# Maxima, sums, division and layout of the early 256-query jobs by matrix products instead of transfers

## The chip, the cores and the metric

The kernel runs on one core of a Trainium2 chip. The metric is the device time of one execution in microseconds (us); the median of three executions of the kernel before is 1216.22 us (1215.47 to 1220.72). One execution was profiled; its trace is what is read below. The engines are TensorE (PE in the rows; PEld is its weight load), VectorE (DVE), ScalarE (ACT), GpSimd (POOL) and SyncE (SP, which only issues transfers here).

## What is computed

Decayed causal attention over 8 batches of 8 heads (576 positions, head size 64), followed by a feed-forward layer with a squared ReLU over the 4608 resulting tokens:

```python
scores = scale * np.matmul(q, k.transpose(0, 1, 3, 2))
cum = np.cumsum(np.log(np.clip(f, 0.0001, 1.0)), axis=-1)
decay = cum[:, :, :, None] - cum[:, :, None, :]
scores = np.where(causal, -1000000000.0, scores + decay)
scores = scores - np.max(scores, axis=-1, keepdims=True)
attn = np.exp(scores)
attn = attn / (np.sum(attn, axis=-1, keepdims=True) + 1e-09)
attn_out = np.matmul(attn, v)            # 8 x 8 x 576 x 64
x = attn_out.transpose(0, 2, 1, 3).reshape(4608, 512)
h = np.maximum(x @ w_in, 0.0)            # 512 -> 2048
out = h * h @ w_out                      # 2048 -> 512
```

All arrays are float32. Most matrix products run on operands split into an upper part (a reduced float32 that TensorE takes in one pass, `fp32r` in the rows) and a lower part (the rest), three products for one.

## The kernel before

**Attention jobs.** The work on attention is cut into jobs. The first eight are LOW jobs: job g takes the queries 0 to 255 of heads 2g and 2g+1 of batches 0 and 1. Then come 16 HIGH jobs (queries 256 to 575 of one head of these two batches), then 48 FULL jobs (a head of the other batches). A job loads q and k (`load`, L542), makes the split operands (`c1` to `c4`, `s1`, `s2`, L590 to L617), puts the cumulated decay in two more rows of the operands (`rows`, L561), and takes the row maxima: a matmul with the queries on the partitions (`mm`, L684, matmul L687) and a masked minimum of the negated scores on VectorE (`top`, L692, L695), one number for each query in a column of the tile `tcol`. The scores are then computed again with the keys on the partitions (`score`, L737, matmuls L739 and L743), where the maxima must lie along a row: `store` (L701, L704) writes the column `tcol` into row 66 of the operand by a transfer. ScalarE takes the exponential out of PSUM (`exp`, L749), GpSimd masks the diagonal block (`mask`, L752), and the products with v follow (`av`, L820; L824 for LOW jobs and batches 0 and 1, in full float32).

**Sums and division.** v has a column of ones, so row 64 of the product is the sum of each query, and the result lies transposed: 64 features on the partitions, queries along the row. ScalarE copies it to `xt` and the sums to `den` (L848, L854). For each pair of jobs `finish` (L889) then gathers the sums into a square tile by a transfer (`cmp<-den`, L901), inverts them on VectorE (L905, L906), stores them in DRAM (L909), spreads them over 64 partitions by two more transfers (L916) and multiplies (`divide`, L929).

**Feed-forward.** Chunks of 256 tokens: chunk c is split into `xh` and `xl` (`chunk`, L967; L977 and L983). Chunks 0 and 1 are the LOW queries of batches 0 and 1. For each of 16 slices of the hidden layer `mlp` (L1003) runs 12 matmuls (`m1`, L1020), ReLU (L1026), the square twice on two paths (`gh`, upper part, ScalarE L1035; `g`, L1030 on ScalarE or L1032 on VectorE), their difference (`gl`, VectorE L1038), and 6 matmuls (`m2`, L1049). While chunk 0 runs, chunk 1 runs beside it with the same slices. The 32 weight slices are loaded by GpSimd and split, mostly on VectorE (`weight`, L410: L427, L431, L438, L444, L309, L452); a slice can be used when its `lower` (L452) is done.

**What sets the order.** Every piece of work is recorded with `add`: its engine or engines with a planned duration, what it comes after, buffers that it takes and gives, and a priority. `Order.run` (L122) plays these durations through and emits the pieces in the order in which they would start; each engine then works through its own list strictly in that order. `SLACK` (L102) is added to the planned end of every piece before another may start on it. Where a piece can run on two engines, the one that would end first is taken (L149). `weight_prio` and `job_prio` set the priorities of weights and jobs, `SETS` and `RAWS` how many jobs may use operand buffers that lie in the place of later weight slices. The loads of q, k and v are issued by ScalarE (`QUEUE`), all other transfers of the attention by SyncE.

## Time and profile before

| | kernel before |
|---|---|
| median of three executions | 1216.22 us |
| the profiled execution: its time | 1220.14 us |
| its span, first to last instruction | 1218.4 us |
| TensorE busy | 1165.4 us (96%) |
| VectorE, ScalarE, GpSimd busy | 790.8, 724.4, 381.0 us |
| mean granted clock of TensorE | 0.983 |

Busy time leaves out the issuing of transfers and waits. The clock is a share of full speed. A group row gives the line of the kernel, engine, operation, output<-input by names, shapes and count, then the busy time in all, the mean duration of one (ns), and the idle time of the engine ahead of it with what ended it. Neighbouring instructions of an engine overlap a little at their ends, so the durations of a stretch sum to more than its busy time. The start of the run is where the engines wait most; from 250 us on TensorE hardly waits.

### The profile page before, as it was taken

To read this page: it belongs to the slowest core of one execution; us is meant where nothing else is said; L and a number is where in the kernel's file an instruction comes from. 1 tells how busy PE (TensorE), PEld (TensorE's weight loads), DVE (VectorE), ACT (ScalarE), POOL (GpSimd) and SP (SyncE) were. 2 spreads that over 40 slices of the span, in tenths; PEclk is the share of its full clock that TensorE was granted. 3 is DMA by queue.
4 is the path that set the end of the run, shared out by engine and by line. 5 is a ranking of instruction groups with operands and counts; after the bars stand their busy time and mean duration, and the time that the engine had idled before them with its cause. 6 is when DMAs were issued, how large, how long until landed. Compare 5 with 4: busy or idle time off the path is not lost.

```text
span 1218.4 us, 23217 instructions
## 1 busy us (share of the span) xinstructions
PE 1165.4 (96%) x7600; PEld 1038.7 (85%) x7600; DVE 790.8 (65%) x2211; ACT 724.4 (59%) x1859; POOL 381.0 (31%) x568
## 2 busy tenths in 40 slices
PE   4679998999999999999999999999999999999998
PEld 4558776789998898999999998899998999999997
DVE  7689988968877677777657674467656753233332
ACT  3566766556766666767777674477746763333232
POOL 3223321245444344544444442045423510000000
PEclk9689999999999999999999999999999999999999
DMA  3654554321222112222212212012211200000000
GB/s 80 140 129 121 143 154 113 87 77 43 65 50 62 40 41 59 47 64 47 59 42 59 42 43 58 19 41 43 69 31 44 47 28 11 18 19 11 8 19 18
DMA packets 122354, 69.85 MB, mean 57 GB/s; under 512 B 101914, under 2 KB 106042, under 8 KB 122234
## 3 DMA queue, kind: packets, MB, share of 16 engines
q10 hardware_dynamic: 53760, 31.47, 10.5%
q1 hardware_dynamic: 63866, 20.12, 7.5%
q0 software_dynamic: 4608, 16.78, 4.4%
q8 instruction: 61, 1.00, 0.3%
q14 instruction: 59, 0.48, 0.1%
HBM read 58.14 MB, written 9.88 MB: 56 GB/s over the span
## 4 chain that ended last, share of the span: by engine, by line
PE 85%; DMA 6%; DVE 4%; ACT 2%; issue 1%; POOL 1%; SPq 0%; ACTq 0%; POOLq 0%; DVEq 0%
PE bank L1049 31%; PE bank L1020 30%; PE bank L739 4%; PE bank L687 4%; PE bank L743 4%; PE bank L824 3%; PE bank L829 3%; PE bank L828 3%; PE bank L827 3%; DMA den<-rdr 2%; DMA cmp<-den 1%; DMA rdr<-cmp 1%; DMA up<-tcol 1%; DVE bank L695 1%; POOL pl L752 0%
## 5 line engine op out<-in xcount | busy, mean ns | idle before, releaser
L1049 PE MATMUL bank<-w,gh 128*128 128x512 f32 x1152 | 413.5, 400 | 1.9 <-DVE w L452 1.9
L1020 PE MATMUL bank<-xh,w 128*128 128x256 f32 x2304 | 324.4, 283 | 2.5 <-DVE xh L977 1.1
L1020 PEld LDWEIGHTS bank<-xh,w 128*128 128x128 f32 x2304 | 302.3, 189 | 13.7 <-DVE xh L977 1.3
L1026 ACT ACTIVATE r<-bank 128x256 f32<-128x256 f32 x288 | 110.2, 383 | 243.3 <-PE bank L1020 220.7
L1049 PEld LDWEIGHTS bank<-w,gh 128*128 128x128 f32 x1152 | 218.0, 189 | 41.8 <-DVE w L452 2.3
L1049 PE MATMUL bank<-w,gl 128*128 128x512 f32 x576 | 228.6, 397 | 0.3 <-DVE gl L1038 0.3
L1032 DVE TENSOR_TENSOR g<-r 128x256 f32<-128x256 f32 x191 | 82.9, 434 | 174.6 <-ACT r L1026 173.3
L1020 PE MATMUL bank<-xl,w 128*128 128x256 f32 x1152 | 182.0, 280 | 0.9 <-DVE xl L983 0.9
L752 POOL TENSOR_SCALAR_AFFINE_SELECT p<-p 128x128 f32<-128x128 f32 (+1 forms) x240 | 84.3, 353 | 307.3 <-ACT p L749 302.0
L695 DVE CUSTOM_DVE_ANT_0 bank<-bank,mz 128x448 f32<-128x448 f32 (+4 forms) x320 | 137.1, 431 | 66.5 <-PE bank L687 64.9
L780 DVE TENSOR_TENSOR pl<-p,ph 128x320 fp32r<-128x320 f32 (+3 forms) x240 | 147.9, 625 | 39.5 <-ACT ph L777 38.4
L1038 DVE TENSOR_TENSOR gl<-g,gh 128x256 fp32r<-128x256 f32 x288 | 139.6, 485 | 51.9 <-ACT g L1030 20.3
L1020 PEld LDWEIGHTS bank<-xl,w 128*128 128x128 f32 x1152 | 155.3, 189 | 1.3 <-DVE xl L983 1.3
L607 POOL TENSOR_TENSOR st<-qkraw,up 64x576 fp32r<-64x576 f32 x96 | 146.2, 1523 | 27.3 <-issue 5.4
L749 ACT ACTIVATE p<-bank 128x320 f32<-128x320 f32 (+4 forms) x288 | 110.0, 389 | 56.5 <-DVE pl L780 30.6
L739 PE MATMUL bank<-up 67*128 67x192 f32 (+3 forms) x364 | 121.8, 335 | 20.4 <-DMA up<-tcol 10.3
L1035 ACT ACTIVATE gh<-r 128x256 fp32r<-128x256 f32 x288 | 120.1, 417 | 31.6 <-PE bank L1049 11.6
L777 ACT CAST ph<-p 128x320 fp32r<-128x320 f32 (+3 forms) x240 | 106.2, 446 | 49.0 <-POOL p L752 27.6
L687 PE MATMUL bank<-up 66*128 66x448 f32 (+1 forms) x352 | 112.1, 322 | 13.0 <-DMA up<-w 9.9
L1049 PEld LDWEIGHTS bank<-w,gl 128*128 128x128 f32 x576 | 109.4, 190 | 15.1 <-DVE gl L1038 1.5
L743 PE MATMUL bank<-st 128*128 128x192 f32 (+3 forms) x364 | 109.3, 302 | 0.0
L739 PEld LDWEIGHTS bank<-up 67*128 67x128 f32 (+1 forms) x364 | 68.5, 188 | 31.5 <-DVE cmp L905 7.2
(102 smaller groups left out, 1612.5 us busy)
## 6 DMA issues: line engine op xcount, KB each, us to landing
qkraw<-in_qk ACTq DMA_DIRECT2D x48, 288.0 KB
v<-in_v ACTq DMA_DIRECT2D x64, 160.0 KB
out<-osb SPq DMA_DIRECT2D x35, 256.0 KB
w<-in_w_in POOLq DMA_DIRECT2D x16, 512.0 KB, 4.4
w<-in_w_out POOLq DMA_DIRECT2D x16, 512.0 KB, 4.6
den<-rdr SPq DMA_DIRECT2D x48, 144.0 KB
up<-tcol SPq DMA_DIRECT2D x232, 0.5 KB
qkraw<-in_qk ACTq DMA_DIRECT2D x11, 224.0 KB
```

The costliest lines, as they stand in the source:

```text
L607: (nc.vector if e == "DVE" else nc.gpsimd).tensor_tensor(out=out, in0=in0, in1=in1.bitcast(F32), op=ALU.subtract,)
L687: nc.tensor.matmul(ps.tile[:m, :n], r2[:D + 2, o + q0:o + q0 + m], kl0[:D + 2, o + k0:o + k0 + n], start=True, stop=True,)
L695: nc.vector.tensor_tensor_reduce(out=ps.tile[:m, :n], in0=ps.tile[:m, :n], in1=mz[:m, mo:mo + n], op0=ALU.add, op1=ALU.min, scale=-1.0, sc ...
L739: nc.tensor.matmul(ps.tile[:kn, :n], kl0[:D + 3, o + k0:o + k0 + kn], r2[:D + 3, o + q0:o + q1], start=True, stop=False,)
L743: nc.tensor.matmul(ps.tile[:kn, :n], l2[:, o + k0:o + k0 + kn], r1[:, o + q0:o + q1], start=False, stop=True,)
L749: nc.scalar.activation(out=pt.tile[:kn, :n], in_=ps.tile[:kn, :n], func=AF.Exp, scale=SCALE)
L780: nc.vector.tensor_tensor(out=pl.tile[:kn, :n], in0=pt.tile[:kn, :n], in1=ph.tile[:kn, :n].bitcast(F32), op=ALU.subtract,)
L1020: nc.tensor.matmul(ph.tile[:, :T], w[:, s, cc], x[:, cc, :], start=(cc == 0 and k == 0), stop=(cc == NCC - 1 and k == 2),)
L1026: nc.scalar.activation(out=r.tile, in_=ph.tile[:, :T], func=AF.Relu)
L1035: nc.scalar.activation(out=gh.tile, in_=r.tile, func=AF.Square)
L1038: nc.vector.tensor_tensor(out=gl.tile, in0=g.tile, in1=gh.tile.bitcast(F32), op=ALU.subtract)
L1049: nc.tensor.matmul(po, x[:, ts], w[:, s], start=(fc == 0 and k == 0), stop=(fc == NF - 1 and k == 2),)
```

## The change

For LOW jobs alone: the negated maxima go into the scores as products of a matrix of ones with a diagonal matrix (the identity `eye` scaled by the column `tcol`), one for each 128 queries. The products with v are turned round, so that queries lie on the partitions and sums in a column beside them; VectorE inverts the column, ScalarE (or VectorE) scales the rows, and a product with the identity turns the result back. `xh` and `xl` are taken from that in PSUM. For all jobs some choices of engine change, a favour of 300 ns against VectorE enters the choice, slacks and priorities are new, and SyncE instead of ScalarE issues the LOW jobs' loads of q, k and v.

```diff
-    SLACK = {"PE": 250.0, "DVE": 200.0, "ACT": 200.0, "POOL": 200.0, "SP": 200.0}
+    SLACK = {"PE": 300.0, "DVE": 250.0, "ACT": 250.0, "POOL": 200.0, "SP": 200.0}
+    FAVOUR = {"PE": 0.0, "DVE": 300.0, "ACT": 0.0, "POOL": 0.0, "SP": 0.0}
...
-                        if way is None or start + busy < way[0] + way[1][1]:
-                            way = start, w
+                        done = start + busy + self.FAVOUR[e]
+                        if way is None or done < way[2]:
+                            way = start, w, done
...
     def weight_prio(i):
-        return (14.9 if i < 4 else 16.9) + 0.8 * i
+        return (10.1 if i < 4 else 15.1) + 0.65 * i
...
-            return 12 + 2 * (g - NLOW)
-        return (30 if g < NLOW + BE * H else 98) + g - NLOW - H
-    SETS = 16
-    RAWS = 14
+            return 8 + 1.5 * (g - NLOW)
+        return (20 if g < NLOW + BE * H else 98) + g - NLOW - H
+    SETS = 14
+    RAWS = 16
...
+    DIRECT = 2
...
+    FIRST = "SP"
...
+    eye = rest[0][:, :P]
+    normal = spare_v.pop().rearrange("p i j d -> p (i j d)")[:, :2 * P]
+    small = spare(16)
+    ones = small[:, :P]
+    diags = [small[:, i * P:(i + 1) * P] for i in range(1, 8)]
...
-            add(("load", g), [dma(260000, QUEUE, 2)], load, [before("load") or "f"], take=[raw], prio=p - 4)
+            add(("load", g), [dma(260000, FIRST, 2)], load, [before("load") or "f"], take=[raw], prio=p - 4)
...
-            elif g == 0:
+            elif g < DIRECT:
...
+                if final and kind == LOW:
+                    dg = dgs[i, q0] = buf("diag", lambda x: diags[x])
+                    def diag(e, t=t, dg=dg):
+                        if e == "ACT":
+                            nc.scalar.activation(out=dg.tile, in_=eye, func=AF.Copy, scale=tcol.tile[:, t:t + 1])
+                        else:
+                            nc.vector.tensor_scalar(dg.tile, eye, tcol.tile[:, t:t + 1], None, ALU.mult)
...
+                if kind == LOW:
+                    nc.tensor.matmul(
+                        ps.tile[:, :n], kl0[:D + 2, o + k0:o + k0 + P], r2[:D + 2, o + q0:o + q1],
+                        start=True, stop=False,
+                    )
+                    for x in range(q0, q1, P):
+                        nc.tensor.matmul(
+                            ps.tile[:, x - q0:x - q0 + P], ones, dgs[i, x].tile, start=False, stop=False,
+                        )
+                    nc.tensor.matmul(
+                        ps.tile[:, :n], l2[:, o + k0:o + k0 + P], r1[:, o + q0:o + q1], start=False, stop=True,
+                    )
...
+    def low_products(g, p, pend, last_av):
...
+                for t in range(QA // P):
+                    for j in range(t + 1):
+                        nc.tensor.matmul(
+                            acc.tile[:, at(i, t)], pend[unit[i, j]][0].tile[:, (t - j) * P:(t - j + 1) * P],
+                            spare_v[g][:, i, j, :D + 1], start=j == 0, stop=j == t,
+                        )
...
+        def invert(e):
+            x = den.tile[:, :4]
+            nc.vector.tensor_scalar_add(x, view()[:, :, D], EPS)
+            nc.vector.reciprocal(out=x, in_=x)
+        def divide(e):
+            if e == "DVE":
...
+            for a in range(4):
+                nc.scalar.activation(
+                    out=out.tile[:, a * D:(a + 1) * D], in_=view()[:, a, :D], func=AF.Copy, scale=den.tile[:, a:a + 1],
+                )
+        def turn(e):
+            for t in range(QA // P):
+                nc.tensor.matmul(
+                    turned.tile[:, t * P:(t + 1) * P], out.tile[:, t * P:(t + 1) * P], eye, start=True, stop=True,
+                )
+        def upper(e):
+            copy(e, xs[b].tile[0][:, g % NPAIR, :], turned.tile[:, :QA])
+        def lower(e):
+            xh, xl = xs[b].tile
+            nc.vector.tensor_tensor(
+                out=xl[:, g % NPAIR, :], in0=turned.tile[:, :QA], in1=xh[:, g % NPAIR, :].bitcast(F32), op=ALU.subtract,
+            )
...
-                add(key, [act(n)] if c < 2 else [dve(n)], upper, need, take=[] if keys else [xs[c]], prio=p)
+                add(key, [act(n), dve(n)], upper, need, take=[] if keys else [xs[c]], prio=p)
```

How this moves the order is shown at three places. The names are those of the tiles; `up`, `st` and `w` hold the split operands (the w tiles are places of later weights), with a number that tells users apart.

On TensorE, where the first LOW job's scores begin, in the kernel before:

```order
L687 MATMUL bank_191<-up_71 128x128
L739 MATMUL bank_202<-up_71 128x256
L743 MATMUL bank_202<-st_77 128x256
L687 MATMUL bank_205<-up_72 128x256
L739 MATMUL bank_211<-up_71 128x128
L743 MATMUL bank_211<-st_77 128x128
```

and in the changed one, where w_86 is the tile of the ones and the diagonals:

```order
L715 MATMUL bank_195<-up_71 128x128
L779 MATMUL bank_202<-up_71 128x256
L784 MATMUL bank_202<-w_86 128x128 x2
L787 MATMUL bank_202<-st_77 128x256
L779 MATMUL bank_211<-up_71 128x128
L784 MATMUL bank_211<-w_86 128x128
L787 MATMUL bank_211<-st_77 128x128
```

The products with the diagonals stand between the two halves of each score, and no transfer of maxima comes ahead of them.

On SyncE's queue, right behind the load of f, before:

```order
L568 DMA up_71<-w_81 1x2x256
L568 DMA up_71<-w_82 1x2x256
L401 DMA cum_dr<-w_81 64x576
L401 DMA cum_dr<-w_82 64x576
L704 DMA up_71<-tcol_177 1x128x1 x2
L570 DMA up_72<-cum_dr 2x2x256
L704 DMA up_71<-tcol_177 1x128x1 x2
L570 DMA w_74<-cum_dr 2x2x256
L704 DMA up_72<-tcol_214 1x128x1 x4
```

and now, where L575 and L665 are the loads of q and k and of v:

```order
L575 DMA qkraw<-in_qk 64x2x256 x2
L575 DMA w_162<-in_qk 64x2x256 x2
L593 DMA up_71<-w_81 1x2x256
L593 DMA up_71<-w_82 1x2x256
L421 DMA cum_dr<-w_81 64x576
L421 DMA cum_dr<-w_82 64x576
L575 DMA w_177<-in_qk 64x2x256 x2
L593 DMA up_72<-w_81 1x2x256
L593 DMA up_72<-w_82 1x2x256
L575 DMA w_216<-in_qk 64x2x256 x2
L597 DMA w_74<-cum_dr 2x2x256
```

The transfers of maxima are gone from this queue, and the loads of later jobs now stand behind the decay rows of earlier ones.

On VectorE, where the sums of the second pair of LOW jobs are inverted, before:

```order
L695 ISA tcol_527 128x1
L929 TENSOR_TENSOR xt_326<-xt_326,den_357 128x2x256
L695 ISA bank_529,tcol_527<-bank_529,mz 128x256
L695 ISA tcol_527 128x1
L309 CAST w_81<-w_457 64x512
L905 TENSOR_SCALAR cmp_531<-cmp_531 128x8
L906 RECIPROCAL cmp_531<-cmp_531 128x8
```

and the first job's inversion, scaling and split now:

```order
L1009 TENSOR_SCALAR tcol_346<-bank_319 128x4
L1010 RECIPROCAL tcol_346<-tcol_346 128x4
L1014 TENSOR_TENSOR w_85<-bank_319,tcol_346 128x256
L723 ISA bank_362,tcol_364<-bank_362,mz 128x256
L723 ISA tcol_364 128x1
L316 CAST st_77<-w_297 64x512
L634 TENSOR_TENSOR st_77<-w_297,up_71 64x512
L723 ISA bank_372,tcol_364<-bank_372,mz 128x128
L723 ISA tcol_364 128x1
L634 TENSOR_TENSOR st_77<-w_297,up_71 64x512
L1035 TENSOR_TENSOR xl_385<-bank_366,xh_384 128x256
```

The inversion now reads the sums out of PSUM, once for each job, and waits for TensorE instead of for a transfer; other work stands between it and the split.

## Rows read from the trace of the kernel before

**Rows 1.** Slices of a fortieth of the span: busy tenths of TensorE, granted clock.
```profile
PE   4679998999999999999999999999999999999998
PEclk9689999999999999999999999999999999999999
```

**Rows 2.** Stretches (us): length, busy time of engines, clock, transfers' share, GB/s.
```profile
0.00:50.00 50.00, 27.00 (x110) 22.23 (x110) 36.16 (x108) 20.34 (x47) 14.77 (x48) 0.87 0.48 116
50.00:100.00 50.00, 39.23 (x203) 30.89 (x202) 41.48 (x114) 33.35 (x87) 12.38 (x31) 0.82 0.48 111
100.00:150.00 50.00, 48.62 (x288) 39.96 (x288) 46.31 (x114) 35.01 (x88) 18.04 (x28) 1.00 0.52 146
150.00:200.00 50.00, 44.35 (x261) 36.23 (x259) 40.11 (x101) 33.26 (x82) 13.32 (x29) 0.97 0.48 135
200.00:250.00 50.00, 46.35 (x259) 37.63 (x260) 45.74 (x124) 27.84 (x71) 13.58 (x22) 0.93 0.31 86
300.00:1000.00 700.00, 696.07 (x4794) 634.58 (x4794) 475.23 (x1372) 474.65 (x1237) 284.96 (x382) 1.00 0.21 48
1000.00:1219.00 219.00, 213.78 (x1369) 192.60 (x1367) 70.66 (x183) 67.98 (x166) 1.42 (x1) 1.00 0.04 14
```

**Rows 3.** The weights' lower parts: count, min/median/max ns, first and last start.
```profile
L452 DVE TENSOR_TENSOR w<-osb,w x32: 666/684/778, 55.3 to 247.4; 128x512 fp32r<-128x512 f32 x32
```

**Rows 4.** Waits of TensorE up to 140 us: in total, times, longest.
```profile
PE bank L739 <- DMA up<-tcol: 10.0, 4, 4.2
PE bank L687 <- DMA up<-w: 9.9, 1, 9.9
PE bank L739 <- DVE cmp L905: 6.6, 2, 4.8
```

**Rows 5.** Waits of VectorE up to 95 us.
```profile
DVE cmp L905 <- DMA cmp<-den: 8.5, 3, 4.1
DVE bank L695 <- PE bank L687: 3.8, 6, 1.0
DVE xt L929 <- DMA den<-rdr: 1.2, 1, 1.2
```

**Rows 6.** TensorE in order of time, first scores: start, duration, wait ahead.
```profile
14.88 0.55 PE L739 MATMUL bank<-up 67*128 67x256 f32 x1 [3.85 <-DMA up<-tcol]
```

**Rows 7.** VectorE by shape, up to 250 us.
```profile
L695 DVE CUSTOM_DVE_ANT_0 bank<-bank,mz 128x256 f32<-128x256 f32 x32 | 13.6, 425 | 10.3 <-PE bank L687 9.5 <-DMA up<-tcol 0.8
L983 DVE TENSOR_TENSOR xl<-xt,xh 128x256 fp32r<-128x256 f32 x12 | 5.0, 439 | 0.1
L309 DVE CAST w<-w 64x512 fp32r<-64x512 f32 x11 | 4.6, 414 | 0.2
L929 DVE TENSOR_TENSOR xt<-xt,den 128x512 f32<-128x512 f32 x4 | 2.7, 681 | 1.2 <-DMA den<-rdr 1.2
L905 DVE TENSOR_SCALAR cmp<-cmp 128x8 f32<-128x8 f32 x4 | 0.7, 185 | 8.5 <-DMA cmp<-den 8.5
```

**Rows 8.** ScalarE by shape, up to 250 us.
```profile
L749 ACT ACTIVATE pl<-bank 128x128 f32<-128x128 f32 x16 | 4.4, 276 | 2.2 <-PE bank L824 1.4 <-PE bank L743 0.5
L749 ACT ACTIVATE pl<-bank 64x64 f32<-64x64 f32 x15 | 3.2, 210 | 0.9 <-PE bank L743 0.8
L1030 ACT ACTIVATE g<-r 128x256 f32<-128x256 f32 x33 | 13.4, 406 | 1.5 <-DVE gl L1038 1.4
```

**Rows 9.** The same square on VectorE, whole span.
```profile
L1032 DVE TENSOR_TENSOR g<-r 128x256 f32<-128x256 f32 x191 | 82.9, 434 | 174.6 <-ACT r L1026 173.3
```

**Rows 10.** ScalarE and its queue's issues, in order of time: start, duration.
```profile
0.80 1.51 ACTq L550 DMA_DIRECT2D qkraw<-in_qk  x2
6.24 0.54 ACTq L550 DMA_DIRECT2D w<-in_qk  x1
9.87 0.62 ACT L309 CAST up<-w 64x512 fp32r<-64x512 f32 x1 [1.72 <-DMA w<-in_qk]
```

**Rows 11.** TensorE's last wait, in the last group of the feed-forward.
```profile
1212.36 0.19 PEld L1049 LDWEIGHTS bank<-w,gl 128*128 128x128 f32 x1 [0.35 <-DVE gl L1038]
```

More of the change, by code (lines that the diff above doesn't have):

```diff
@@ L458, in weight @@
         splits = ("c1", "c2", "c3", "c4", "s1", "s2")
-        if 17 <= i < 20:
-            after += [("avs", NLOW - 1)]
+        if 16 <= i < 20:
+            after += [("turn", g) for g in range(NLOW)]
         elif 20 <= i < 24:
@@ L759, in job @@
             need.append(("score", g, u - 1) if u else ("score", g - 1, len(jobs[g - 1]["units"]) - 1) if g else None)
-            add(("score", g, u), [pe(n, n)], score, need, take=[ps], give=[operands], prio=p - 0.3)
+            give = [dgs[i, x] for x in range(q0, q1, P)] if kind == LOW else []
+            add(("score", g, u), [pe(n, n, *[P] * len(give))], score, need, take=[ps], give=[operands] + give, prio=p - 0.3)
             add(("exp", g, u), [act(n)], exp, [("score", g, u)], take=[pt], give=[ps], prio=p - 0.5)
@@ L800, in job @@
             uses[u] = uses.get(u, 0) + 1
-        both = bank("av") if kind == LOW else None
         den = st["den"] = (
@@ L832, in job @@
             n = s1_ - s0
-            take = [acc] if first and (kind != LOW or i == 0) else []
+            take = [acc] if first else []
             give = [x for x in (ph, pl) if x]
@@ L836, in job @@
             need = need + [last_av] + ([("v", g)] if whole else [("vl", g)])
-            if whole and kind != LOW:
+            if whole:
                 need.append(("ones", g))
@@ L861, in job @@
                 m = QA if low else S - QA
-                take = [xts[b]] if h % H == 0 and i == 0 and (kind == LOW or kind == FULL and not low) else []
+                take = [xts[b]] if h % H == 0 and not low else []
                 kx = ("x", g, i, low)
@@ L967, in chunk @@
     def chunk(c):
+        if c < BE:
+            return [("xl", c * NPAIR + i) for i in range(NPAIR)]
         keys = []
```

173 lines of the change are left out of this document (99 added, 74 removed).

## The prediction

> **What bounds the kernel now.** Read the slices first [rows 1]: TensorE is at 4, 6 and 7 tenths in the first three and at 8 or 9 from the fourth on, and its granted clock dips only there. The stretches give the sizes [rows 2]. From 300 to 1000 us TensorE is busy 696.07 of 700 us, and from 1000 us to the end 213.78 of 219, where about 5 us are the last copies and stores. So nothing that the change does after 300 us can win much: what can be won lies in the first 250 us, where TensorE is busy 205.55 of 250 us.
>
> What holds it there? VectorE is busy 209.80 of the same 250 us, ScalarE 149.79. VectorE's largest task is to split the 32 weight slices, and the last of them is finished by 247.4 us and its own 0.68, so at 248.1 us [rows 3]. TensorE saturates then for good. So I take the moment at which the last weight slice is ready as the clock of this stage: the sum asks how much earlier it comes. VectorE's idle time before it is about 40 us (250 less 209.8): 22.4 us in the first 100 us (13.84 and 8.52), 17.8 in the rest.
>
> The waits say what stands behind that. TensorE waits 10.0 us for the maxima on their way into the operand, 6.6 us behind VectorE's inversion, and 9.9 us at the start for the decay rows [rows 4]. VectorE itself sits 8.5 us, in three waits, until the gathered sums arrive, 1.2 us for the spread ones, and 3.8 us, in six, for TensorE [rows 5].
>
> **Part by part.** The sum is made against the profiled execution, 1220.14 us with a span of 1218.4; it lies 3.92 us above the median of the runs, and I take that off at the end.
>
> *VectorE's work up to the last weight slice.* I count both orders up to the last `lower`. Gone: 12 casts of 64x512 at 0.414 us (5.0), five more casts of about 0.4 (2.0), four divisions at 0.681 (2.7), eight small inversion instructions at 0.19 (1.5), 16 `xl`, eleven of them at 0.439 and five smaller ones (6.0), nine `xh` casts of about 0.25 (2.2), two `gl` of about 0.43 (0.9); together 20.3 us. New: eight `xl` out of PSUM, which no row shows; the maximum pass over 256 columns of PSUM takes 0.425, the same subtraction in SBUF 0.439, so 3.4. Sixteen small inversion instructions at 0.19 (3.0), five diagonals between 0.19 and 0.414, taken at 0.2 (1.0), one scaling (0.4), two casts of 576 columns (0.9), and three maxima of one more job that now stands ahead (2.0); together 10.7 [rows 7]. The net is -9.6 us of summed durations; neighbours overlap, so I count **-8.0**. All lies on the path, since VectorE's order is strict.
>
> *VectorE's waits.* The gather and the spread go, so 8.5 and 1.2 us go [rows 5]: **-9.7**. What is late next: each of the eight inversions waits for TensorE, each `xl` for ScalarE's `xh`, and behind a waiting instruction stand the next maxima, casts and weight steps, for which TensorE and ScalarE wait in turn. No row shows these 16 waits. The nearest are the six for TensorE, 0.6 us each: so between 0, if the work ordered in between covers them, and 10. In the piece of VectorE's order shown with the change eight instructions stand between the scaling and the `xl` of the first job, so I take a small value, **+2.0**.
>
> *The maxima.* Of the 32 transfers of LOW maxima the first costs 3.85 us of TensorE's time [rows 6]; a scaling on ScalarE and two products replace it. Later jobs overlap one another, so of the 10.0 us I count only what also starves VectorE at the start: **-1.5**, between 0 and -3.85.
>
> *ScalarE.* 27 diagonals are 128 columns (0.276 us by the exponential of that size) and 28 scalings of 64 columns (0.210): 13.3 us more, against 24 copies of 256 or 512 columns that go (at the 0.406 of a pass over 256 columns, 9.7 us) and 32 issues of loads of 0.54 to 0.75 [rows 8, 10]. ScalarE is idle or issuing for 46 of the first 100 us [rows 2], so this is hidden and counts nothing; uncovered it would be 4 us. The Trainium skill ("ScalarE: Activation LUTs", What ACT_TABLE_LOAD costs) adds about 93 ns to an ACTIVATE for each operand that it takes from a column, as these 55 do for their scale; by its figure they cost an estimated 5.1 us more, and if nothing covered them the forecast would be 5 us later. No row here has an ACTIVATE with such a scale.
>
> *TensorE.* The LOW products with v had 16 x (256 + 128) = 6144 columns in full float32; now 48 x 65 and, for the turning, 16 x 128 make 5168. 48 products of 128 columns with diagonals are new. Even at 1.2 GHz, the lower level of the clock, 128 columns are an estimated 0.11 us, 5 us in all, in a stretch where TensorE is idle for 23 of 50 us [rows 2]: nothing, with 5 us as the bound. Both orders put 30 groups of the second feed-forward product ahead of the first use of the last weight, so an earlier weight really is an earlier end.
>
> *SyncE.* 32 issues of loads move to its queue, in front of and behind the decay rows, and 32 transfers of maxima and 16 of the division leave it. The queue gets shorter; its waits are the third rival.
>
> *The end.* 174 squares `g` go from VectorE to ScalarE. The two take 0.434 and 0.406 us [rows 8, 9], so the load only changes sides; but `gh` and `g` now follow each other on ScalarE where they ran side by side. That is covered by a product group until the last one, which waits 0.35 us for its `gl` already [rows 11]: **+0.4**.
>
> Sum: -8.0 - 9.7 + 2.0 - 1.5 + 0.4 = -16.8 us, so 1203.3 us for an execution like the profiled one, and less 3.92 for the median: **1199 us**. With the unknown waits between 0 and 10 and the first maxima between 0 and -3.85 the sum lies between about -7.5 and -21; an own range of 1193 to 1208.
>
> **The rivals.**
>
> *A larger gain.* The idle time of VectorE is contagious: in the first 100 us all but 9 us of start (TensorE has done its first maxima at 11.0 us, 14.88 less the wait of 3.85 [rows 6]) may close, 13 us, and since chunk 1's feed-forward no longer waits for the second half of the jobs, a quarter of the later 17.8 too, some 5. With -8.0 that is -26: 1190 us. For it speaks that both the gather and the column transfers stood in series with the same eight jobs; against it that loads and decay rows remain transfers.
>
> *A smaller gain.* The waits are replaced one for one; only the -8.0 remains: 1208 us. For it speaks that the chain of a job through four engines in strict order grows by a step of each.
>
> *The change doesn't shorten the early jobs.* SyncE issues strictly in order, and a load of job g+2 stands behind the decay rows of job g, which wait until its operand is written. ScalarE issued a load at 6.24 us, and its data let the cast start at 9.87, 3.6 us later [rows 10]; the first wait for decay rows lasted until 9.9 us [rows 4]. If two jobs share a round of load, cast and rows, and a round takes between 6 and 11 us, eight jobs take 24 to 44 us. At the upper end the loads set the pace, the transfers removed were hidden behind them anyway, and their waits come back elsewhere, with part of the 8.0: 1214 us.
>
> *Slower: ScalarE becomes the bound.* The squares put 174 x 0.406 = 70.6 us on ScalarE, and 42 casts of operands of later jobs and 50 of `xh` come to it too, some 45 us. From 300 to 1000 us it is busy 474.65 of 700 us [rows 2], and in strict order. About 100 of the squares lie between 250 and 1000 us. If each of them holds up TensorE's second product by more than 0.17 us, the 17 us are gone; at 0.35 us, most of a square's length, it is +35 - 17: 1234 us. Against it: ScalarE would still have a fifth of that time free, and the end of the run, where it is busy 67.98 of 219 us, takes the rest without harm. The Trainium skill ("ScalarE: Activation LUTs", Rules for kernel authors) says to multiply on VectorE, not ScalarE, for its speed in bf16; for this float32 square the trace doesn't agree, 434 against 406 ns [rows 8, 9].
>
> **How the numbers follow.** The forecast 0.42, the larger gain 0.20, the smaller 0.18, no shorter jobs 0.10, slower 0.10. About 0.5%, 6 us, is what a measurement of this kernel can tell from no change: faster is below 1210.1, slower above 1222.3. The forecast and the larger gain are faster, of the smaller nearly all (0.16), together 0.78. No change is the rest of it, the case without shorter jobs and a mild form of the last, 0.13. Slower is 0.09. The range reaches from within the larger gain to the middle of the third rival: 1185 to 1214, leaving out a part of the larger gain and the slower case, about 2 in 10.
>
> **What would show it.** Right: the last weight's `lower` starts near 231 us instead of 247.4; VectorE has no wait for a gather in the first 90 us and some 30 us idle before that `lower`; TensorE passes 7 tenths a slice earlier; TensorE stays above 99% from 300 to 1000 us; and the tail after the last weight is as long as before. The larger gain: the last `lower` near 222. The third rival: ScalarE or VectorE waiting for `in_qk` in each early job. The slower case: TensorE waiting for `gl` behind ScalarE's `g` hundreds of times after 300 us. The forecast is wrong at its root if the last weight is much earlier and the end isn't, for then this stage was not what set it.

## The result and the profile after

The changed kernel is slower: 1222.1 us in the median (1218.74 to 1224.32) against 1216.0 for the kernel before on the same chip, a ratio of 1.0048 (95% interval 1.003 to 1.0066). 1199 us was forecast, and 1185 to 1214 as the range. By the bounds that the prediction set itself (slower above 1222.3) that is only just no change, to which it gave 0.13; the interval excludes 1 all the same. The profiled execution took 1221.07 us with a span of 1219.4.

First the page of the changed kernel: busy time by engine, then the slices of TensorE and its granted clock, as in [rows 1].

```profile
PE 1188.7 (97%) x7712; PEld 1068.0 (88%) x7712; DVE 699.4 (57%) x1921; ACT 831.0 (68%) x2190; POOL 372.4 (31%) x571
PE   6999999999999999999999999999999999999998
PEclk9999999999999999999999999999999999999999
```

TensorE is at 9 tenths from the second slice on, two slices sooner than before. That looks like the forecast come true, and it is the trap of this case: a fuller engine that does more. Its busy time rose from 1165.4 us to 1188.7, with 112 products more. The stretches, in the columns of [rows 2] (length; PE, PEld, DVE, ACT, POOL busy; clock; transfers):

```profile
0.00:50.00 50.00, 37.84 (x170) 36.74 (x171) 31.42 (x99) 31.52 (x83) 13.95 (x51) 1.00 0.40 108
50.00:100.00 50.00, 47.46 (x240) 42.77 (x240) 36.69 (x108) 31.70 (x88) 9.43 (x27) 0.97 0.36 102
100.00:150.00 50.00, 47.40 (x277) 37.68 (x277) 44.05 (x114) 34.52 (x89) 15.99 (x30) 1.00 0.49 130
150.00:200.00 50.00, 45.47 (x256) 35.34 (x254) 43.05 (x110) 30.37 (x78) 12.21 (x27) 0.97 0.44 124
200.00:250.00 50.00, 46.53 (x257) 36.37 (x256) 42.59 (x100) 33.54 (x83) 18.30 (x30) 0.97 0.42 110
300.00:1000.00 700.00, 699.80 (x4817) 640.66 (x4817) 423.92 (x1193) 528.97 (x1411) 281.01 (x378) 1.00 0.21 48
1000.00:1219.00 219.00, 215.41 (x1381) 194.52 (x1379) 40.40 (x104) 102.77 (x259) 3.59 (x5) 1.00 0.04 14
```

In the first 100 us VectorE is busy 68.11 us where it was 77.64: it has less to do and gets to it later. From 300 to 1000 us TensorE is busy 699.80 of 700 us, 3.7 us more than before. So the loss that this trace shows lies ahead of that, and the weights' lower parts, the clock that the forecast used, show it (columns as in [rows 3]):

```profile
L472 DVE TENSOR_TENSOR w<-osb,w x32: 669/686/1347, 68.3 to 253.8; 128x512 fp32r<-128x512 f32 x32
```

The last one starts at 253.8 us, 6.4 us later than before [rows 3], where 231 was forecast. What follows it is 5.4 us shorter (965.6 us to the end of the span against 971.0). So the two traces differ by 1.0 us in all, where the medians differ by 6.1: the profiled execution before lies 4.1 us above that median and this one 1.0 below its own. Where the other 5 us lie, no trace shows. VectorE's waits up to 95 us (in total, times, longest) say who is late:

```profile
DVE bank L723 <- PE bank L715: 13.6, 12, 2.2
DVE tcol L1009 <- PE bank L988: 9.5, 7, 3.1
```

The waits for the gather and the spread of [rows 5] are gone, 9.7 us; 23.1 us for TensorE stand in their place, where 3.8 were. And TensorE, up to 140 us, hardly waits after its start (compare [rows 4]):

```profile
PE bank L715 <- DMA up<-w: 9.0, 2, 8.5
PE bank L784 <- ACT w L746: 2.7, 1, 2.7
PE bank L791 <- DMA up<-tcol: 2.3, 1, 2.3
```

So the early stage is bound by TensorE. By what in it, the loads of weights in order of time tell (start, duration, instructions). Lines 988 are products of probabilities with values, line 1122 is the feed-forward's first product:

```profile
28.31 0.97 PEld L988 LDWEIGHTS bank<-w,ph 128*128 128x128 f32 x4
29.16 0.55 PEld L988 LDWEIGHTS bank<-w,pl 128*128 128x128 f32 x2
...
70.72 1.83 PEld L1122 LDWEIGHTS bank<-xh,w 128*128 128x128 f32 x8
72.44 0.97 PEld L1122 LDWEIGHTS bank<-xl,w 128*128 128x128 f32 x4
...
74.04 0.30 PEld L988 LDWEIGHTS bank<-w,pl 128*128 128x128 f32 x2
74.26 0.19 PEld L791 LDWEIGHTS bank<-up 67*128 67x128 f32 x1
```

At 28 us four loads take 29.16 - 28.31 = 0.85 us, 0.213 each, and at 70.72 eight take 1.72, 0.215 each. The moving operand has 65 columns in the first case and 256 in the second, and the load sets the pace of both. Where the columns take longer than the load, they set it. In the kernel before, at 1.2 GHz, the old products with values loaded 65 columns and moved 256 of float32 in two passes (TensorE's own rows, start, duration, instructions):

```profile
47.33 1.06 PE L824 MATMUL bank<-ph,w 128*65 128x256 f32 x2
48.18 0.63 PE L824 MATMUL bank<-pl,w 128*65 128x128 f32 x2
```

The two passes took 48.18 - 47.33 = 0.85 us, 0.427 each. In the early jobs of the changed kernel the load sets the pace of all products. At 74 us two loads take 0.22 us, 0.11 each, so here the clock has doubled. The Trainium skill ("TensorE: Matmul & The Clock Gate", LDWEIGHTS) gives a load as its columns over 1.2 in nanoseconds, an estimated 107 for 128; the trace agrees at 74 us and shows twice that at 28.

An early job now issues 4 products for its maxima, 8 for scores, 6 with diagonals, 12 records for the values (six products of float32 in two passes) and 4 for the turning: 34 loads, 34 x 0.213 = 7.2 us, and eight jobs 58 us. TensorE has them behind it at some 73 us, and until then it is full.

The granted clock reads 1.00 there all the same. The changed kernel's stretch from 30 to 40 us, and below it that of a run that is told of later, which differs by 20 idle products at the start:

```profile
30.00:40.00 10.00, 10.00 (x49) 10.00 (x48) 5.95 (x25) 6.39 (x23) 1.69 (x6) 1.00 0.11 25
```

```profile
30.00:40.00 10.00, 10.00 (x49) 10.00 (x49) 5.95 (x25) 6.02 (x21) 1.67 (x6) 0.50 0.06 15
```

The same 49 products fill the same 10 us, once recorded at 1.00 and once at 0.50. In the second run the records hold a rise and a fall before 20 us; in the first no change is recorded until the feed-forward has begun, and the column shows full speed until then. The pitch, 0.213 or 0.11 us for a load of 128 columns, tells the level where the column can't: 1.2 GHz. The column of the kernel before [rows 1] is as blind at the start: its first record, a rise, comes at 30.5 us, and its loads of 128 columns stand 0.213 us apart until then.

### The profile page after: what moved, and what is told of

The parts are those of the page before. It is cut to its first block, busy times and chain, and to the rows that moved or that the text cites. A ratio compares the mean times of both kernels' runs of the same rounds, so it can differ in the third digit from the quotient of the medians.

```text
span 1219.4 us, 23317 instructions
## 1 busy us (share of the span) xinstructions
PE 1188.7 (97%) x7712; PEld 1068.0 (88%) x7712; DVE 699.4 (57%) x1921; ACT 831.0 (68%) x2190; POOL 372.4 (31%) x571
## 4 chain that ended last, share of the span: by engine, by line
PE 91%; DMA 3%; DVE 2%; ACT 1%; issue 1%; POOL 1%; SPq 0%; POOLq 0%; ACTq 0%; DVEq 0%
PE bank L1122 32%; PE bank L1151 32%; PE bank L715 5%; PE bank L791 4%; PE bank L795 4%; PE bank L882 3%; PE bank L881 3%; PE bank L880 3%; PE bank L877 2%; DMA up<-tcol 2%; PE bank L988 2%; DVE bank L723 1%; PE bank L784 1%; PE bank L787 1%; PE bank L779 1%
## 5 line engine op out<-in xcount | busy, mean ns | idle before, releaser
L1140 DVE TENSOR_TENSOR gl<-g,gh 128x256 fp32r<-128x256 f32 x288 | 152.4, 529 | 274.6 <-ACT gh L1137 211.4
L804 POOL TENSOR_SCALAR_AFFINE_SELECT p<-p 128x128 f32<-128x128 f32 (+1 forms) x240 | 81.8, 342 | 374.8 <-ACT p L801 368.8
L833 DVE TENSOR_TENSOR pl<-p,ph 128x320 fp32r<-128x320 f32 (+3 forms) x240 | 143.6, 603 | 39.7 <-ACT ph L830 38.6
L830 ACT CAST ph<-p 128x320 fp32r<-128x320 f32 (+3 forms) x240 | 106.4, 446 | 40.5 <-PE bank L795 13.2
L715 PE MATMUL bank<-up 66*128 66x256 f32 (+1 forms) x360 | 114.0, 322 | 11.7 <-DMA up<-w 9.0
L791 PE MATMUL bank<-up 67*128 67x192 f32 (+2 forms) x358 | 117.2, 327 | 7.0 <-DMA up<-tcol 4.4
L1132 ACT ACTIVATE g<-r 128x256 f32<-128x256 f32 x271 | 111.5, 411 | 4.6 <-DVE gl L1140 0.8
L795 PE MATMUL bank<-st 128*128 128x192 f32 (+2 forms) x358 | 105.2, 294 | 0.0
L791 PEld LDWEIGHTS bank<-up 67*128 67x128 f32 (+1 forms) x358 | 64.6, 180 | 18.5 <-issue 6.3
```

The source lines that it names most:

```text
L715: nc.tensor.matmul(ps.tile[:m, :n], r2[:D + 2, o + q0:o + q0 + m], kl0[:D + 2, o + k0:o + k0 + n], start=True, stop=True,)
L791: nc.tensor.matmul(ps.tile[:kn, :n], kl0[:D + 3, o + k0:o + k0 + kn], r2[:D + 3, o + q0:o + q1], start=True, stop=False,)
L795: nc.tensor.matmul(ps.tile[:kn, :n], l2[:, o + k0:o + k0 + kn], r1[:, o + q0:o + q1], start=False, stop=True,)
L833: nc.vector.tensor_tensor(out=pl.tile[:kn, :n], in0=pt.tile[:kn, :n], in1=ph.tile[:kn, :n].bitcast(F32), op=ALU.subtract,)
L1132: nc.scalar.activation(out=g.tile, in_=r.tile, func=AF.Square)
L1140: nc.vector.tensor_tensor(out=gl.tile, in0=g.tile, in1=gh.tile.bitcast(F32), op=ALU.subtract)
```

## The experiments

Each ratio is to runs of the kernel before on the same chip, in five rounds, with its 95% interval. My theory: the early stage is bound by small products that cost a load of weights each at 1.2 GHz. Rivals: ScalarE, to which the change gives 107 us of work; and the settings (order, priorities, queues), which the change alters as well.

### Which part of the change costs

Four runs cut the change into its settings, the diagonals for the maxima, and the small products for sums, division and layout. The settings alone, over the kernel before, are all that the pieces shown with the change alter from `SLACK` to `FIRST`, the last line there, and what those pieces leave out: a slack of 800 ns behind the gathers of the later jobs, other choices of engine for the casts of q and k, and a later start of the weights (behind the fourth load of v instead of the second).

> The kernel before with every setting of the change that isn't the products with diagonals and the identity: the planner's slack and favour, the priorities, the queue of the first loads, two jobs' rows sent directly, the numbers of sets and raw parts. The early jobs compute as before. Small products (theory): 1211 to 1217 us, no loss. Settings (rival): 1221 to 1224 us, the loss is there already. ScalarE (rival): the favour of 300 for VectorE's load moves the copies and casts to ScalarE here as well, so about 1220 to 1224 us.

1228.3 us, 1.0107 (1.009 to 1.0124). The rival was nearer, but not in its own way: the last weight starts at 246.4 us, sooner than before. What is lost comes later, from 350 to 450 us, where TensorE is busy 100.00 us in the changed kernel. This run's stretch, and its largest wait there:

```profile
350.00:450.00 100.00, 93.30 (x631) 84.40 (x630) 65.72 (x183) 75.82 (x198) 48.16 (x63) 0.95 0.22 50
```

```profile
PE bank L834 <- DVE pl L787: 4.8, 5, 1.8
```

In this order the products with values stand where VectorE has not yet split their probabilities, and the clock dips behind the waits: 631 products where the changed kernel has 695 in the same time.

The settings with the diagonals (line 746 and the products of line 784), sums and division as before:

> The same settings, and the diagonals in the scores (6 more small products per early job) in place of the column transfers of the maxima; sums, division and layout of the early jobs stay as before, by the old products of 256 columns, the gather and the spread. Small products (theory): 8 x 6 x 0.213 = 10 us of products more on TensorE than with the settings alone, but the wait for the column transfers (10.0 us) goes: about the time of the settings alone, within 4 us, and under the changed kernel's. ScalarE (rival): as the settings alone plus the diagonals that ScalarE writes, 1222 to 1225 us. Settings (rival): the same time as with the settings alone.

1212.3 us, 0.9978 (0.9963 to 0.9993): a version under both kernels. The theory had put it under the changed kernel, but within 4 us of the settings alone; it lies 16 below. The diagonals alone, with the old settings:

> The kernel before, with the old settings, and the diagonals for the maxima alone. Additive parts (theory): 1215 - 16 = 1199 us. Fit (rival: the diagonals repair what the new settings broke, a wait for column transfers that now comes sooner): 1209 to 1215 us, not faster than with the new settings (1212).

1228.8 us, 1.0098 (1.0069 to 1.0128). And the changed kernel with its diagonals taken out:

```
-                if final and kind == LOW:
+                if False:
...
-                if kind == LOW:
-                    nc.tensor.matmul(
+                if False:
+                    nc.tensor.matmul(
```

> The changed kernel with the maxima of the early jobs sent as before, by column transfers, and no diagonals; sums, division and layout stay with the small products. Additive parts (theory: settings cost +13 us, diagonals give 16 back, the small products for sums and layout cost 10): 1228 + 10 = 1238 us. Fit (rival: the settings cost nothing by themselves, they only don't fit a stage that still waits for the gather): 1218 to 1224 us, since here the gather is gone.

1215.2 us, 0.9984 (0.9965 to 1.0002). Parts that add up would have given 1238; settings that merely don't fit the old stage would have let the diagonals gain under the old ones. Neither holds: the diagonals cost 13 us with one set of settings and save 16 with the other. With the new settings each half of the change alone saves 13 to 16 us over the settings, and both together only 6.

The traces, one for each, say where. The last weight starts at 246.4 us with the settings alone, at 247.2 with the diagonals, at 249.1 with the small products and at 253.8 with both. The rest of the span is 980.8 us with the settings alone, and 963.3, 965.4 and 965.6 us in the other three, in which TensorE is busy for 99.2 us or more from 350 to 450 us. So what each half saves over the settings is the stall there, which is gone. In the early stage each half costs, and the two together cost more (7.4 us) than the sum of both (3.5). Two changes that take each other's room on one engine behave so, but a new order may as well, and the settings, which mostly reorder, cost 13 us by themselves. So the runs that decide keep the order.

### The small products, with the order kept

The changed kernel without its 48 products with diagonals, so without the maxima in the early scores; ScalarE and VectorE still write the diagonals.

> The changed kernel without the 48 products with diagonals (the maxima are left out of the scores of the early jobs; the diagonals are still written by ScalarE or VectorE). Small products (theory): 48 x 0.213 = 10.2 us less on TensorE, 1212 to 1216 us. Settings (rival): 1222 us.

1209.9 us, 0.9948 (0.993 to 0.9966). Then the six products with values in one pass, where float32 takes two, with ones in place of the values, so that this version leaves the attention's result out:

```
-  pt = buf(..., named(..., [P, 448], F32))
+  pt = buf(..., named(..., [P, 448], F32R if kind == LOW else F32))
...
-  spare_v[g][:, i, j, :D + 1], start=j == 0, stop=j == t,
+  ones[:, :D + 2], start=j == 0, stop=j == t,
```

> The changed kernel with the six products of probabilities and values of an early job in one pass of the reduced type instead of two passes of float32: 6 x 8 = 48 loads of weights fewer in the early stage. The values are replaced by ones there, since those are at hand in the reduced type; ScalarE, VectorE and the settings have the same work as in the changed kernel. Small products (theory): 48 x 0.213 = 10.2 us of TensorE's early time go, so 1212 us, as without the small products for sums and layout; at least 1216 if other waits take part of it. Settings (rival): 1222 us, no difference.

1208.9 us, 0.9934 (0.9911 to 0.9958). Both forecasts said 10.2 us of TensorE's time less, and 12.2 and 13.2 came, which the intervals (some 2 us to either side of each time) don't tell apart; every other instruction of every engine stands in the order of the changed kernel. The first recorded rise of the clock comes at 65.6 and 69.5 us instead of 73.9, so the early jobs ran at the lower level here too. The last weight's start moves with it, first without diagonals, then in one pass, against 253.8:

```profile
L472 DVE TENSOR_TENSOR w<-osb,w x32: 676/686/1351, 60.2 to 245.3; 128x512 fp32r<-128x512 f32 x32
```

```profile
L472 DVE TENSOR_TENSOR w<-osb,w x32: 676/686/1357, 59.4 to 241.7; 128x512 fp32r<-128x512 f32 x32
```

A third way takes 16 products out and leaves the arithmetic: a head's two diagonals side by side, so that a unit of 256 queries needs one product of 256 columns.

```
-  for x in range(q0, q1, P):
-      nc.tensor.matmul(ps.tile[:, x - q0:x - q0 + P], ones, dgs[i, x].tile, ...)
+  nc.tensor.matmul(ps.tile[:, :n], ones, dgs[i].tile[:, q0:q1], ...)
```

> The changed kernel with the two diagonals of a head side by side, so that the first unit of a head takes one product of 256 columns where it had two of 128: 2 x 8 = 16 products fewer, with the same arithmetic. Small products (theory): if each costs a load of weights, 16 x 0.213 = 3.4 us less, so 1218 to 1219 us; if columns counted and not loads, no change, 1222 us. Settings (rival): 1222 us.

1229.7 us, 1.0106 (1.007 to 1.0141), a miss that says nothing of the products: three buffers instead of seven gave the planner another order, the last weight starts 6 us sooner (247.8), and the stall from 350 to 450 us is back:

```profile
350.00:450.00 100.00, 92.86 (x606) 83.70 (x606) 69.72 (x186) 75.20 (x199) 47.25 (x64) 0.93 0.22 48
```

```profile
PE bank L881 <- DVE pl L834: 4.8, 6, 1.8
```

With the planner told of the same seven buffers, the order stays:

> The changed kernel with the two diagonals of a head side by side and 16 products fewer, as in the paired run, but with the buffers told to the planner as before, so that the order on every engine is that of the changed kernel. Small products (theory): the paired run lost its gain to another order (TensorE waits from 350 to 450 us), not to the products; with the order kept, 16 x 0.213 = 3.4 us less, 1217 to 1220 us. Rival (a product of 256 columns costs as much as two of 128): 1222 us.

1217.8 us, 1.0007 (0.999 to 1.0025): 4.3 us less than the changed kernel where 3.4 were expected.

### The clock

Twenty products on unused data at the start, while TensorE waits, in the changed kernel and in the one before:

```
+    def warm_up(e):
+        for _ in range(20):
+            nc.tensor.matmul(warm_bank.tile[:, :MW], mz[:, MW - P:], mz, start=True, stop=True)
```

> The changed kernel with 20 products of 448 columns more, on data that nothing uses, at the start, while TensorE waits for its first operands; all else is as it was. Small products (theory): the early stage of the changed kernel is bound by some 34 weight loads per early job at 0.213 us each, which is the pitch at 1.2 GHz; at the other level it would be half. If the clock rises before the first early job and stays up, 8 x 34 x 0.107 = 29 us of TensorE's early time goes; what VectorE and ScalarE then set leaves some 10 to 15 us of that, so 1207 to 1212 us, and the last lower part of a weight ends at 239 to 244 us instead of 253.8. If the clock falls again under the small products, 1222 us, as without. ScalarE (rival: the work that moved from VectorE to it is what costs): no difference, 1222 us. Settings (rival: the order of work, priorities and queues that were changed with it cost the time): no difference, 1222 us.

> The kernel before with the same 20 products at the start. Small products (theory): its early jobs have only some 24 loads' worth of TensorE time and wait for VectorE and the column transfers, so a higher clock takes off less than in the changed kernel: 1212 to 1216 us. ScalarE and settings (rivals): both say nothing of the clock, 1216 us.

1226.5 us, 1.0098 (1.008 to 1.0116), no gain but a loss of some 4 us, which the traces don't explain, and 1213.4 us, 0.9985 (0.9972 to 0.9998), a small gain. In the changed kernel the clock rose and had fallen again by 20 us; from 20 to 70 us it is granted 0.50 throughout, with TensorE busy for 49.54 of the 50 us (a stretch of it is shown above). Next, 30 products in front of the second early job's scores, when TensorE is already full:

> The changed kernel with 30 products of 256 columns more, whose results are written over, ahead of the first scores of the second early job, when TensorE is already busy without a gap: 30 x 0.213 = 6.4 us at most. Small products with a held clock: if the clock rises in the burst and the small products behind it keep it, seven jobs take half of 7.2 us each, 25 us less on TensorE, of which other engines leave about half: 1207 to 1215 us. Small products that don't hold the clock: it falls back to 1.2 GHz behind the burst, and the burst is lost time: 1225 to 1229 us. Settings (rival): 1222 us plus the burst, the same.

1226.3 us, 1.0076 (1.0048 to 1.0104). Its loads in order of time, line 780 being the burst:

```profile
17.70 4.88 PEld L780 LDWEIGHTS bank<-st 128*128 128x128 f32 x30
...
22.62 0.31 PEld L786 LDWEIGHTS bank<-w 128*128 128x128 f32 x2
22.85 0.19 PEld L789 LDWEIGHTS bank<-st 128*128 128x128 f32 x1
...
26.31 0.30 PEld L786 LDWEIGHTS bank<-w 128*128 128x128 f32 x2 [1.09 <-ACT w L746]
26.52 0.19 PEld L789 LDWEIGHTS bank<-w,w 128*128 128x128 f32 x1
26.64 0.53 PEld L990 LDWEIGHTS bank<-w,ph 128*128 128x128 f32 x4
...
28.00 0.97 PEld L990 LDWEIGHTS bank<-w,ph 128*128 128x128 f32 x4
```

The clock rises inside the burst (30 loads in 4.8 us), and behind it loads stand 0.11 us apart. It falls at about 27.3 us, after the first products with values and after a wait of 1.09 us. Which of the two? The next edit keeps every load and the order, and widens the moving side of those products from 65 columns to 128 by reading the values twice. They are read from the second column on, so this version leaves the first column of values out and doesn't give the attention's result; it is there for its time:

```
-        C = D + 2
+        C = 2 * D
...
-  spare_v[g][:, i, j, :D + 1], start=j == 0, stop=j == t,
+  spare_v[g][:, i, j, 1:D + 1].unsqueeze(1).broadcast_to([P, 2, D]), start=j == 0, stop=j == t,
```

> The changed kernel with the six small products of probabilities and values of an early job made 128 columns wide instead of 65, by giving the values twice; the same number of weight loads, the same order on every engine. (The values are shifted by one column, so that the sums still come out of the last one.) Columns hold the clock (theory): a wide product costs no more than a small one, since the load of weights sets the pitch, but TensorE now computes through it; if that lets the clock rise in the early stage, 1205 to 1214 us. Number of products alone (rival): no difference, 1222 us. If wide products are dearer than the load: 1225 us or more.

1205.3 us, 0.9907 (0.9882 to 0.9931): 17 us less than the changed kernel, for more columns. With the burst in front:

> The same wide products together with the burst of 30 products ahead of the second early job. With small products behind it, the burst raised the clock by about 20 us and it fell by 27.4 us, within the first products of probabilities and values. Columns hold the clock (theory): it stays at 2.4 GHz through the early stage, 1207 to 1214 us in spite of the burst. Waits break the clock (rival: two short waits of TensorE, 0.2 and 0.9 us, came just before the fall): it falls at the same place, 1226 us as with the burst alone.

1210.6 us, 0.9942 (0.992 to 0.9964). The burst isn't needed and costs 5 us. But the run tells the two causes apart, for the same wait stands at the same place:

```profile
26.07 0.30 PEld L786 LDWEIGHTS bank<-w 128*128 128x128 f32 x2 [1.10 <-ACT w L746]
...
27.41 0.53 PEld L990 LDWEIGHTS bank<-w,ph 128*128 128x128 f32 x4
```

After a wait of 1.10 us the four loads at 27.41 us stand 0.11 us apart, and the clock is recorded at the higher level from 20.9 to 75.6 us. So that wait alone doesn't bring it down; with the narrow products behind it, it fell.

### ScalarE

The planner's favour for VectorE set to zero gives the casts and squares back to VectorE:

```
-    FAVOUR = {"PE": 0.0, "DVE": 300.0, ...}
+    FAVOUR = {"PE": 0.0, "DVE": 0.0, ...}
```

> The changed kernel with the planner's favour of 300 for VectorE's load set to zero, so that copies and casts go back from ScalarE to VectorE where the planner finds VectorE free. ScalarE (rival): if the 107 us of work that moved to ScalarE cost time, 1216 us or under. Small products (theory): TensorE's early products stay, so 1222 us, or a few us more where VectorE is late with the early jobs (1220 to 1228 us).

1227.3 us, 1.0085 (1.0051 to 1.0118): no gain, rather a loss. The planner makes another order of it, so this run alone would not settle the matter; but the rival's own row says the same: TensorE was busy 699.80 of 700 us while ScalarE carried the squares.

### Towards a better version

The version with the settings and the diagonals alone, with the diagonals side by side, and with the 20 products at the start:

> The version with the settings and the diagonals alone (sums, division and layout as before), with the diagonals of a head side by side: 16 products fewer. Small products (theory): TensorE is not the bound of its early stage (it is idle 26 of the first 100 us), so little, 1210 to 1213 us, and still under both kernels. If each product counted there too: 1209 us. Settings (rival): 1212 us.

> The version with the settings and the diagonals alone, which was at 1212 us, with 20 products at the start. As in the kernel before, whose early jobs also have TensorE waiting: 2 us less, 1209 to 1211 us. If the clock falls at the first wait behind them and that is all: 1212 us.

1212.6 us, 0.9964 (0.9945 to 0.9983), and 1212.8 us, 0.9967 (0.995 to 0.9984). In this version, where TensorE is idle for 26 of the first 100 us, neither fewer products nor an early rise of the clock pays.

The wide products so that everything is computed: two overlapping windows of 64 columns, the second of which ends on the ones, so the sum comes out in column 127.

```
+        def twice(x):
+            return bass.AP(x.tensor, x.offset, [x.ap[0], (1, 2), (1, D)])
...
-  spare_v[g][:, i, j, :D + 1], start=j == 0, stop=j == t,
+  twice(spare_v[g][:, i, j, :D + 1]), start=j == 0, stop=j == t,
```

> The changed kernel, computing all that the reference does, with the products of probabilities and values 128 columns wide: the 64 values, and 64 columns that begin one later and end on the ones, so that the sum of the probabilities stands in the last. Loads of weights and order as in the changed kernel. Columns hold the clock (theory): as with the shifted values, 1203 to 1209 us, faster than both kernels. Number of products alone (rival): 1222 us.

> The same with the two diagonals of a head side by side (16 products fewer, order kept). Small products: 16 x 0.213 = 3.4 us at 1.2 GHz, or half at 2.4 GHz. With the clock up, TensorE is no longer without a gap in the early stage (8.6 to 9.1 of 10 us busy from 30 to 60 us in the run with shifted values), so 0 to 2 us less than the wide version: 1203 to 1208 us. If TensorE were still the bound: 3 us less.

1206.2 us, 0.9919 (0.99 to 0.9939), and 1205.5 us, 0.9913 (0.989 to 0.9935): both faster than both kernels, and the paired one by no more than was expected. The loads of the first of them in order of time, line 991 being the products with values:

```profile
22.34 0.97 PEld L991 LDWEIGHTS bank<-w,ph 128*128 128x128 f32 x4
23.19 0.55 PEld L991 LDWEIGHTS bank<-w,pl 128*128 128x128 f32 x2
...
28.28 0.54 PEld L991 LDWEIGHTS bank<-w,ph 128*128 128x128 f32 x4
28.74 0.30 PEld L991 LDWEIGHTS bank<-w,pl 128*128 128x128 f32 x2
...
34.52 0.97 PEld L991 LDWEIGHTS bank<-w,ph 128*128 128x128 f32 x4
...
40.04 0.53 PEld L991 LDWEIGHTS bank<-w,ph 128*128 128x128 f32 x4
```

Four loads take 0.85 us at 22 us and 0.46 at 28: the clock has risen within the early jobs. Among the early jobs it drops once, at 32.9 us, behind waits of 0.63 and 0.50 us, and is back at 36 us without a burst. Its last weight, and VectorE's waits up to 95 us:

```profile
L472 DVE TENSOR_TENSOR w<-osb,w x32: 674/686/1204, 56.7 to 239.1; 128x512 fp32r<-128x512 f32 x32
```

```profile
DVE bank L723 <- PE bank L715: 8.7, 8, 2.8
DVE tcol L1012 <- PE bank L991: 4.7, 3, 3.2
```

## Why the prediction was wrong

The step that failed is TensorE's: "nothing, with 5 us as the bound". It failed three times over.

- *The price.* It took 128 columns at 1.2 GHz as 0.11 us. A product of the early jobs costs 0.213 there, its load of 128 columns, be its own columns 65, 128 or 256. By columns the values' products looked like a saving (5168 for 6144); by time a job's eight old passes are an estimated 2.6 us (two times 0.853 and 0.427), and its 16 new ones 3.4.
- *The cover.* It hid the products in the 23 of 50 us in which TensorE was idle [rows 2]. That idle time was TensorE waiting within a job's chain, and the chain was what the change shortens: with the waits gone the idle time goes too, and the jobs stand back to back. Job by job, 12 loads at 0.213 and two times 0.853 and 0.427 us for the old products with values, an estimated 5.1 us, became 7.2: 2.1 x 8 = 17 us more on the engine that now sets the pace.
- *The clock.* The forecast took the low clock of the early stage as given for a dear product, and didn't ask what the new mix does to it. Before, loads ran at the high level from about 31 us to a wait at 37, and at times later; in the changed kernel not before 73 us.

The runs with the order kept show the price, uncovered: 48 loads less made 12.2 and 13.2 us less. What the lower level costs comes out at 16 us by the pair of runs that differ in nothing but the width of the products (1222.1 and 1206.2). With that for TensorE in place of nothing, the sum of -16.8 is about zero; the 6 us by which the kernel came out above that are of the size of the second term that failed, VectorE's waits.

The other steps:

- *VectorE's work*, -8.0: up to the start of the last `lower` VectorE is busy 207.51 us before and 201.08 after, -6.4. Right. In the same time it is idle 39.9 us before and 52.7 after, +12.8, and the two make up the 6.4 us by which that weight is later.
- *VectorE's waits*, -9.7 and +2.0: the 9.7 went. The new waits for TensorE, taken as 2.0 and bounded by 10, are 23.1 - 3.8 = 19.3 us up to 95 us. In the version with wide products they are 13.4 - 3.8 = 9.6, inside the bound; and by the 7.6 that this is over 2.0 the forecast of 1199 would have missed that version's 1206 too. This second term was too small by itself: VectorE's inversion and maxima wait for TensorE at either clock.
- *The first maxima*, -1.5: a wait of 2.7 us for the diagonal where 3.85 stood, -1.15. Right.
- *ScalarE at nothing*: right; it is busy 63.22 of the first 100 us, and TensorE waits for it 3.2 us before the feed-forward, 2.7 of them for the diagonal just named and 0.5 for a scaling. The prices were low: a diagonal took 0.405 us and a scaling 0.318, where 0.276 and 0.210 were taken.
- *The end*, as long as before: the rest after the last weight is 5.4 us shorter in these two traces, and TensorE is busy for 3.7 us more of the 700 from 300 us on. Not foreseen, and in the change's favour.
- *SyncE's queue*, a rival: not seen. No early job of the changed kernel shows ScalarE or VectorE waiting for `in_qk`.
- *The slower case* was given to ScalarE, for which the run without favour and 699.80 of 700 us leave nothing. The engine that became the bound was the one that the forecast watched for being idle.
- *Slips that move little*: the piece of VectorE's order has seven instructions between the scaling and the `xl`, not eight, and the sum's bounds of -7.5 and -21 make 1195 to 1209 us, not 1193 to 1208.

What the views offered in time: PEld stands beside PE in [rows 2], 22.23 us for 110 loads, 0.202 each, in a stretch whose products have different widths. Counting the loads of a job and multiplying, 34 x 0.202 x 8, would have given 55 us of TensorE's time. The Trainium skill ("Perfetto Trace Analysis", Identifying the Most-Contended Engine) calls the products' busy share a poor measure of how near TensorE is to its limit, and takes the useful operations and the loads' busy share instead. Here both shares are full from 20 to 70 us (49.54 and 49.05 of 50 us in the changed kernel), and the runs with loads taken out show that the loads set the pace.

Left open: why the chip grants the higher level to one mix of products and not to the other. The runs show that width alone, at the same loads and order, moves it; they don't show what the chip goes by. Open too is whether 48 loads less really gave 2 to 3 us more than their 10.2, or noise did. Why the settings with the old stage stall from 350 to 450 us was read from the waits and not tried.

## What to carry to other kernels

Price a small product by its load of weights at the level of clock that the stage really has, and count products, not columns, unless the columns take longer than the load. Before calling an idle engine cover for new work, ask whether its idle time belongs to the chain that is being shortened. And where a planner sets the order, compare versions whose order is the same, or a stall elsewhere will be read as the price of the edit: here the two paired runs, the same products in two orders, lie 12 us apart.

## What was not expected of the hardware

- A product with a load of 128 columns took 0.213 us at 1.2 GHz, with 65 or 128 moving columns in a pass of float32 or 128 or 256 of the reduced type, and 0.11 to 0.12 at 2.4. A pass of float32 over 256 columns took 0.427 at 1.2 GHz, though its load had 65 columns.
- TensorE was granted 0.50 for 50 us on end while it was busy for 49.54 of them (the changed kernel with 20 products at the start). With 128 columns instead of 65 in 96 passes of the changed kernel's products the clock rose by 26 us, and the kernel became 16 us faster for doing more.
- The clock column read 1.00 through a stretch whose pitch was that of 0.50, since no change had been recorded yet.
